# A gated mix of sliding attention and a GEGLU feed-forward: who makes the low parts of the hidden products

## The chip, the cores and the metric

The kernel runs on one core of a Trainium2 chip. The metric is the device time of one execution in microseconds (us). TensorE (PE) multiplies, VectorE (DVE) works on elements, ScalarE (ACT) copies and evaluates functions, GpSimd (POOL) and SyncE (SP) issue DMAs here. Each engine takes its instructions in the order of its own queue.

## The reference

```python
g = sigmoid((x * gate_w).sum(-1, keepdims=True))
a = attention(x, wqkv, wo)     # 32 heads of 16; query s sees keys s, s-2, ..., s-14; softmax; times wo
b = (gelu(x @ w_gate) * (x @ w_up)) @ w_down
out = g * a + (1 - g) * b
```

x has 2048 tokens of 512 channels, the feed-forward part (FFN) 1792 hidden features; all is float32.

## The kernel before

The tokens are taken in two parities (even and odd positions, `par` 0 and 1) of 1024 each, since the attention's step of 2 never mixes them. For each parity the program makes keys, queries and values, then the FFN in 14 chunks (`f`) of 128 hidden features. At the end of the second parity the results of the attention are multiplied by `wo` (`out_first` for the first parity, `finish` for the second) and the sums are stored.

Every float32 operand of a matmul is split: a high part is a rounded copy (`hh = Copy(ge)`), a low part what is left (`hl = ge - hh`), and a product is the sum of three matmuls, high by high, low by high and high by low. In the FFN the products of gate and up are made by a scheme of seven block products in place of eight. `gate_up` makes them for a chunk: PE's matmuls stand in line 781, ACT copies sums out of PSUM at L786, L792 and L867, DVE adds them at L793, ACT applies GELU at L882 and L898. PSUM has four banks with the tag `p` and four `acc` banks. `hidden` then multiplies GELU and up on DVE (L797) and makes the two parts, for two halves of the tokens per chunk. It has two ways. In the first, ACT makes the high part (L800) and DVE subtracts it (L801). In the second, ACT writes the negated value, rounded, to the low part (L805), POOL issues a DMA that adds the value to it in place (L806), and ACT makes the high part (L807). The table `LOWS` (line 40) names the chunks of each parity that take the second way. `down` multiplies the parts of earlier chunks by the down weights (PE L830); ACT brings half of the sums back into a PSUM bank before (L824) and out of it after (L845).

The attention is the filling. For each of 8 units (parity, 128 channels) DVE multiplies queries and keys (L539) and reduces (L542), subtracts the maximum (L553, L555), ACT takes the exponential (L557, with a load of its function table before it, and another before the next GELU), DVE normalizes (L562 to L568). `mix` then works through pairs of tokens: a product with the values `v` (L585), three additions (L589, L591, L593), and after every two pairs a transpose (L598), whose result goes to memory by SP (L600). The values come by L523 and L524 into one buffer. `channels` fetches a result from memory (L1040), ACT makes its high part (L90) and DVE its low part (L91). The two parts of `wo` are made at L135 (ACT) and L91. In `finish` PE multiplies them at L1062; ACT and DVE copy the sums out (L1111, L1109), SP stores them (L1115).

The order of all this is not written by hand: a scheduler lays out each engine's queue by its own estimate of when each instruction can run. The attention's instructions are handed in with a lower priority (`tc.high_priority(offset=-BEHIND)`), as many between two products as a budget allows (`pull`). There are six buffers each of `hh` and `hl`, and four `c` tiles hold GELU, up and their products.

Of the kernel before, what the change touches and what calls it, by code (L numbers as in the profile page):

```python
# [36 lines left out]
PIPE = 4  # L37
BT = 4
MASKED = -1e9 * DH ** 0.5
LOWS = (4, 8, 10), (4, 6, 8, 10, 12)  # L40


GROUPS = (("t1", "t2", "b11"), ("b21", "t3", "b22", "t4"))
# [5 lines left out]
def tile_gated_mix(ctx: ExitStack, tc: tile.TileContext, xt, wqkv, wff, wo, out):  # L49
# [11 lines left out]
    def tl(tag, dt=F32):  # L61
        return pool.tile([P, COLS.get(tag, 512)], dt, name=tag, bufs=BUFS[tag])
# [733 lines left out]
    def hidden(par, key, ge, up):  # L796
        nc.vector.tensor_tensor(ge, ge, up, op=OP.mult)  # L797
        hh_, hl_ = tl("hh", F32R)[:, :512], tl("hl", F32R)[:, :512]
        if key[0] not in LOWS[par]:
            END[:] = [nc.scalar.activation(hh_, ge, AF.Copy),  # L800
# [555 lines left out]
```

## Time and profile before

| | |
|---|---|
| time, median of 3 runs | 592.74 us (592.54 to 600.27) |
| profiled execution, time and span | 592.89 us, 591.1 us |
| PE busy | 585.7 us (99%) |
| DVE busy | 535.0 us (91%) |
| ACT busy | 425.3 us (72%) |
| POOL busy | 126.8 us (21%) |
| DMA | 141.71 MB, mean 240 GB/s |

The span is the time from the first to the last instruction that the profile holds; the profiled execution's own time is 1.79 us longer. In a row of the timeline the first number is the start in us from the span's start, the second the time until the end of the instruction, then engine, line, operation, result and operands; a bracket tells how long the engine was idle before it and what ended that. In a row of groups the numbers after the bar are the sum in us and the mean in ns.

### The profile page before, as it was taken

The page shows a single profiled execution, that of the slowest core. Times are in us where ns is not written, and L with a number is a line of the kernel's source. Part 1 is how long each engine was busy: PE and PEld are TensorE (multiplying, and loading weights), DVE is VectorE, ACT ScalarE, POOL GpSimd, SP SyncE. Part 2 cuts the span into 40 slices and gives each one's busy share as a digit, 9 for nine tenths or more (in the row PEclk, how much of TensorE's full clock was granted, in tenths as well). Part 3 has the DMA queues.
Part 4 walks back from the last instruction along what each step waited for, and adds up shares of the span by engine and source line. Part 5 has one row for each costly group of instructions (what it writes and reads, how often), then busy time and mean ns, then how long its engine had stood idle before and what let it go on. Part 6 is the DMA issues. An engine that isn't in the chain of part 4 may idle for free.

```text
span 591.1 us, 8266 instructions
## 1 busy us (share of the span) xinstructions
PE 585.7 (99%) x2743; PEld 489.1 (83%) x2743; DVE 535.0 (91%) x628; ACT 425.3 (72%) x752; POOL 126.8 (21%) x153
## 2 busy tenths in 40 slices
PE   9999999999999999999999999999999999999997
PEld 7889888888888888888889888888888888887885
DVE  6989998999899995998997999998999899989882
ACT  6778667778887779786687655768776967796522
POOL 0140751112111212113120761112121212112200
PEclk9999999999999999999999999999999999999999
DMA  8789999978987979899989999969798989548915
GB/s 305 228 247 281 301 310 231 296 197 238 289 222 218 273 205 273 224 264 347 284 231 380 222 272 269 277 162 257 178 263 224 254 213 247 144 111 227 202 44 178
DMA packets 87848, 141.71 MB, mean 240 GB/s; under 512 B 8575, under 2 KB 49919, under 8 KB 87806
## 3 DMA queue, kind: packets, MB, share of 16 engines
q1 hardware_dynamic: 65454, 103.21, 52.2%
q0 software_dynamic: 22064, 37.59, 34.6%
q8 instruction: 21, 0.34, 0.2%
q10 hardware_dynamic: 288, 0.39, 0.2%
q14 instruction: 21, 0.17, 0.1%
HBM read 69.83 MB, written 46.49 MB: 197 GB/s over the span
## 4 chain that ended last, share of the span: by engine, by line
PE 96%; ACT 2%; DMA 1%; issue 0%; SPq 0%; DVE 0%; ACTq 0%
PE p L781 44%; PE p L830 13%; PE acc L830 12%; PE acc L478 11%; PE p L1062 6%; PE p L364 4%; PE acc L364 3%; PE p L478 2%; PE acc L1062 2%; DMA raw<-xt 1%; ACT A L90 0%; ACT L898 0%; ACT g L135 0%; ACT hl L805 0%; ACT hh L807 0%
## 5 line engine op out<-in xcount | busy, mean ns | idle before, releaser
L781 PE MATMUL p<-S,g 128*128 128x512 f32 x672 | 167.0, 389 | 0.0
L781 PEld LDWEIGHTS p<-S,g 128*128 128x128 f32 x672 | 125.8, 188 | 25.8
L781 PE MATMUL p<-A,g 128*128 128x512 f32 x504 | 125.8, 389 | 0.0
L781 PEld LDWEIGHTS p<-A,g 128*128 128x128 f32 x504 | 94.4, 188 | 19.8 <-ACT rt L845 0.4
L585 DVE TENSOR_TENSOR prod<-v,lg 128x2048 f32<-128x2048 f32 x32 | 72.8, 2274 | 1.4 <-DMA v<-vs 1.2
L542 DVE TENSOR_REDUCE lg<-prod 128x128 f32<-128x2048 f32 x32 | 73.0, 2280 | 0.2
L539 DVE TENSOR_TENSOR prod<-kq 128x2048 f32<-128x2048 f32 x32 | 72.9, 2277 | 0.2
L830 PE MATMUL p<-d,hh 128*128 128x512 f32 x224 | 68.6, 390 | 0.3 <-ACT p L824 0.3
L830 PE MATMUL acc<-d,hh 128*128 128x512 f32 x224 | 59.7, 389 | 0.0
L740 POOL DMA_DIRECT2D g<-raw x26 | 23.6, 907 | 161.1 <-ACT g L737 103.6
L792 ACT ACTIVATE c<-p 128x512 f32<-128x512 f32 x56 | 33.4, 597 | 33.7 <-PE p L781 33.6
L830 PEld LDWEIGHTS p<-d,hh 128*128 128x128 f32 x224 | 41.9, 188 | 9.5 <-ACT p L824 0.8
L830 PEld LDWEIGHTS acc<-d,hh 128*128 128x128 f32 x224 | 42.0, 188 | 8.7
L793 DVE TENSOR_TENSOR c<-c,s 128x512 f32<-128x512 f32 x56 | 37.8, 681 | 5.5 <-ACT c L792 5.2
L830 PE MATMUL p<-d,hl 128*128 128x512 f32 x112 | 42.1, 389 | 0.0
L797 DVE TENSOR_TENSOR c<-c 128x512 f32<-128x512 f32 x56 | 38.1, 683 | 1.3 <-ACT c L898 1.2
L589 DVE TENSOR_TENSOR prod<-prod 128x1024 f32<-128x1024 f32 x32 | 39.0, 1217 | 0.1
L845 ACT ACTIVATE rt<-p 128x512 f32<-128x512 f32 x48 | 27.8, 596 | 15.0 <-PE p L830 14.8
L786 ACT ACTIVATE s<-p 128x512 f32<-128x512 f32 x56 | 33.2, 594 | 5.3 <-PE p L781 4.9
L478 PE MATMUL acc<-d,S 128*128 128x512 f32 x144 | 35.5, 390 | 0.1
L830 PE MATMUL acc<-d,hl 128*128 128x512 f32 x112 | 35.1, 389 | 0.0
L772 POOL DMA_DIRECT2D d<-r x23 | 19.8, 860 | 68.9 <-ACT d L771 41.6
(222 smaller groups left out, 1062.3 us busy)
## 6 DMA issues: line engine op xcount, KB each, us to landing
g<-raw POOLq DMA_DIRECT2D x26, 512.0 KB, 6.7
ws<-g SPq DMA_DIRECT2D x14, 768.0 KB, 5.9
g<-ws SPq DMA_DIRECT2D x14, 768.0 KB, 6.7
r<-wff SPq DMA_DIRECT2D x28, 256.0 KB, 4.4
raw<-wff SPq DMA_DIRECT2D x14, 512.0 KB, 4.6
d<-r POOLq DMA_DIRECT2D x23, 256.0 KB, 6.7
ws<-raw SPq DMA_DIRECT2D x14, 384.0 KB, 5.8
raw<-ws SPq DMA_DIRECT2D x14, 384.0 KB, 4.0
```

What stands on the lines that cost most here:

```text
L364: LAST[:] = [nc.tensor.matmul(ps[:, :n], x[:, ts], VO[b][w][:, kc * WQ:kc * WQ + n], start=first, stop=(kc == 1 and i == 2), skip_group_ch ...
L478: LAST[:] = [nc.tensor.matmul(ps, x[:, ts], w, start=(start and kc == i == 0), stop=(kc == 1 and i == 2), skip_group_check=True)]
L539: paced(nc.vector.tensor_tensor(prod, spans(k, jj), q[:, jj:jj + 2, None, :].to_broadcast([P, 2, W, UC]), op=OP.mult))
L542: nc.vector.tensor_reduce(two_of(lg, jj), prod.rearrange("p j w (h d) -> p (j w) h d", d=DH), axis=AX.X, op=OP.add)
L585: paced(nc.vector.tensor_tensor(prod.rearrange("p j w (h d) -> p (j w) h d", d=DH), spans(v, jj).rearrange("p j w (h d) -> p j w h d", d=D ...
L589: nc.vector.tensor_tensor(prod[:, :, :4], prod[:, :, :4], prod[:, :, 4:], op=OP.add)
L781: LAST[:] = [nc.tensor.matmul(ps, w_, a_, start=(start and kc == 0 and n == 0), stop=(kc == 1 and n == 2), skip_group_check=True)]
L792: nc.scalar.activation(c, ps, AF.Copy)
L793: nc.vector.tensor_tensor(c, c, s, op=OP.add)
L797: nc.vector.tensor_tensor(ge, ge, up, op=OP.mult)
L830: LAST[:] = [nc.tensor.matmul(pp, a[:, ts], w, start=(i == 0 and n == 0 and gr == 0), stop=(i == 1 and n == 2), skip_group_check=True)]
L1062: LAST[:] = [nc.tensor.matmul(pa, a, b, start=(first and n == 0), stop=(last and n == 2), skip_group_check=True)]
```

## The change

The table names no chunk of the second parity any more, so that there every chunk takes the first way of `hidden`.

```diff
-LOWS = (4, 8, 10), (4, 6, 8, 10, 12)
+LOWS = (4, 8, 10), ()
```

Five chunks with two halves make ten low parts. For each, the negated copy (L805) and the adding DMA (L806) go, the copy for the high part is L800 where it was L807, and DVE gets a subtraction (L801). The scheduler lays the queues out anew from chunk 4 of the second parity on; the order of all before is the same.

DVE's queue in the last chunk, from the last L801 on. In the names, `hl`, `hh` and `raw` are parts and data of results of the attention, `prod`, `o` and `tb` the steps of `mix`, `v_4789` and `v_4783` the values of the last unit but one, `v_5298` and `v_5288` those of the last unit. Before:

```order
L801 TENSOR_TENSOR hl_5351<-c_5347,hh_5350 128x512
L585 TENSOR_TENSOR prod_5202<-v_4789,lg_4287 128x2048
L91 TENSOR_TENSOR hl_5533<-raw_5530,hh_5532 128x4x4x32
L91 TENSOR_TENSOR hl_5568<-raw_5530,hh_5567 128x4x4x32
L91 TENSOR_TENSOR hl_5600<-raw_5530,hh_5599 128x4x4x32
L589 TENSOR_TENSOR prod_5202<-prod_5202 128x2x512
L591 TENSOR_TENSOR prod_5202<-prod_5202 128x2x256
L593 TENSOR_TENSOR o_5150<-prod_5202 128x4x64
L598 STREAM_TRANSPOSE tb_5033<-o_5150 128x512
L585 TENSOR_TENSOR prod_5303<-v_5298,lg_4792 128x2048
```

And now, the same place:

```order
L801 TENSOR_TENSOR hl_5341<-c_5337,hh_5340 128x512
L91 TENSOR_TENSOR hl_5523<-raw_5520,hh_5522 128x4x4x32
L598 STREAM_TRANSPOSE tb_5025<-o_5026 128x512
L585 TENSOR_TENSOR prod_5143<-v_4783,lg_4285 128x2048
L91 TENSOR_TENSOR hl_5558<-raw_5520,hh_5557 128x4x4x32
L91 TENSOR_TENSOR hl_5590<-raw_5520,hh_5589 128x4x4x32
L589 TENSOR_TENSOR prod_5143<-prod_5143 128x2x512
L591 TENSOR_TENSOR prod_5143<-prod_5143 128x2x256
L593 TENSOR_TENSOR o_5142<-prod_5143 128x4x64
L585 TENSOR_TENSOR prod_5193<-v_4783,lg_4285 128x2048
```

After the last row shown follow L589, L591, L593, L598 and then the first L585 on the last unit's values. So behind the last L801 there stands one more pair of the unit before the last, and one more transpose, and the three L91 have moved ahead of the L585 that frees the buffer of the values.

ACT's queue in the last chunk, from one L824 to the next (`p_5289` and `p_5279` are the bank of the first). Before:

```order
L824 ACTIVATE p_5289<-rt_3956 128x512
L786 ACTIVATE s_5235<-p_5179 128x512
L135 ACTIVATE S_5237<-raw_5048 128x512
L135 ACTIVATE S_5250<-raw_5048 128x512
L90 ACTIVATE A_5319<-raw_5262 128x4x4x32
L882 ACTIVATE c_5259<-p_5186 128x512
L90 ACTIVATE A_5337<-raw_5262 128x4x4x32
L805 ACTIVATE hl_5225<-c_5221 128x512
L807 ACTIVATE hh_5224<-c_5221 128x512
L824 ACTIVATE p_5324<-rt_3981 128x512
```

And now:

```order
L824 ACTIVATE p_5279<-rt_3956 128x512
L786 ACTIVATE s_5225<-p_5170 128x512
L135 ACTIVATE S_5227<-raw_5040 128x512
L557 ACT_TABLE_LOAD
L557 ACTIVATE lg_4786<-lg_4786 128x512
L135 ACTIVATE S_5240<-raw_5040 128x512
L90 ACTIVATE A_5309<-raw_5252 128x4x4x32
L882 ACT_TABLE_LOAD
L882 ACTIVATE c_5249<-p_5177 128x512
L90 ACTIVATE A_5327<-raw_5252 128x4x4x32
L800 ACTIVATE hh_5215<-c_5212 128x512
L824 ACTIVATE p_5314<-rt_3981 128x512
```

The exponential of the last unit (`lg_4786`) and the two table loads that go with it now stand between the two; before, the exponential stood 13 rows ahead of the first of them, the load back to GELU four rows ahead.

SP's queue at the end, as a difference (`os_134` is the last result of the attention, `s` and `rt` hold sums to be stored):

```order
 L1040 DMA raw<-os_133 128x512
 L600 DMA os_134<-tb 32x4x128 x4
-L1040 DMA raw<-os_134 128x512
 L1115 DMA out<-s 128x512
 L1115 DMA out<-rt 128x512
+L1040 DMA raw<-os_134 128x512
 L1115 DMA out<-s 128x512
 L1115 DMA out<-rt 128x512
```

The fetch of the last result now stands behind the first two stores of sums.

## The prediction

> **What bounds the kernel now.** I read the page's header and chain first, then the engines by stage, then the end of the span on VectorE (DVE), the DMA queue of SyncE (SP) and TensorE (PE).
>
> ```profile
> span 591.1 us, 8266 instructions
> PE 96%; ACT 2%; DMA 1%; issue 0%; SPq 0%; DVE 0%; ACTq 0%
> 350.00:550.00 200.00, 199.67 (x882) 164.98 (x881) 190.12 (x197) 148.79 (x247) 36.75 (x42) 1.00 0.85 219
> 550.00:591.00 41.00, 37.28 (x165) 30.54 (x163) 26.34 (x30) 14.91 (x25) 3.44 (x4) 1.00 0.53 138
> ```
>
> After the stretch and its length the columns are PE, PE's weight load, DVE, ScalarE (ACT), GpSimd (POOL), granted clock, DMA share and GB/s. Nearly the whole chain is matmuls, and in the stretch where the edit lies (350 to 550 us) PE misses 0.33 of 200 us at clock 1.00. So nothing that is taken off another engine there can bring more than 0.33 us. DVE is the second engine: busy 190.12 of 200 us, against ACT's 148.79. The edit loads the engine that is nearly full and relieves two that have room. The profiled execution took 592.89 us (1.79 outside the span), 0.15 over the median of 592.74; I sum against it.
>
> **What the edit removes and adds.** Chunks 4, 6, 8, 10 and 12 of the second parity have two GELU products each, so ten low parts change their way.
>
> ```profile
> L801 DVE TENSOR_TENSOR hl<-c,hh 128x512 fp32r<-128x512 f32 x40 | 27.2, 684 | 2.2 <-ACT hh L800 2.1
> L806 POOL DMA_DIRECT2D hl<-c x16 | 15.1, 942 | 83.1 <-ACT hl L805 82.8 <-DMA r<-wff 0.2
> L805 ACT ACTIVATE hl<-c 128x512 fp32r<-128x512 f32 x16 | 10.0, 628 | 0.0
> 450.22 1.29 DVE L801 TENSOR_TENSOR hl<-c,hh 128x512 fp32r<-128x512 f32 x2
> ```
>
> Removed: ten negated copies on ACT (0.63 us each by their row), ten POOL issues (0.94 us) and ten adding DMAs of 256 KB. All of it lay beside PE's work, POOL being busy 36.75 of 200 us and ACT 148.79, so I take the gain as 0, between 0 and the 0.33 us that PE misses. Added: ten subtractions of 0.684 us on DVE. Two in a row take 1.29 us together, so the second adds 0.60; ten are **6.0 us of DVE time**.
>
> The Trainium skill has a rule against such a step: "Perfetto Trace Analysis", section Optimizing Scalar/DVE Operations, says that some work may be better off on ScalarE when VectorE is saturated, which speaks against this edit. The trace agrees in part: VectorE at 190.12 of 200 us is near it, but with its 9.9 us idle not there, so by the rule alone the 6.0 us would fit and the sum would be 0.
>
> **Where the 6.0 us lie.** DVE is idle for 9.9 of the 200 us; three waits for the exponential of the attention hold most of what other work could fill.
>
> ```profile
> 411.55 0.69 DVE L562 TENSOR_REDUCE m<-lg 128x64 f32<-128x512 f32 x1 [2.22 <-ACT lg L557]
> 465.58 0.69 DVE L562 TENSOR_REDUCE m<-lg 128x64 f32<-128x512 f32 x1 [1.66 <-ACT lg L557]
> 520.41 0.69 DVE L562 TENSOR_REDUCE m<-lg 128x64 f32<-128x512 f32 x1 [1.44 <-ACT lg L557]
> ```
>
> They are 5.3 us. But DVE runs in its queue's order, and the change's order, with each row at its duration, has nearly the old amount of DVE work ahead of each FFN step (from 4 us less to 5 us more, mostly under 1.5), and the attention later instead. After the last L801 there now stand one more pair of tokens of mix (L585, L589, L591, L593) and one more transpose (L598) than before. I count that tail row by row.
>
> ```profile
> 543.48 0.69 DVE L801 TENSOR_TENSOR hl<-c,hh 128x512 fp32r<-128x512 f32 x1
> 544.08 2.28 DVE L585 TENSOR_TENSOR prod<-v,lg 128x2048 f32<-128x2048 f32 x1
> 546.28 1.89 DVE L91 TENSOR_TENSOR hl<-raw,hh 128x512 fp32r<-128x512 f32 x3
> 552.49 2.29 DVE L585 TENSOR_TENSOR prod<-v,lg 128x2048 f32<-128x2048 f32 x1 [1.25 <-DMA v<-vs]
> 557.26 2.29 DVE L585 TENSOR_TENSOR prod<-v,lg 128x2048 f32<-128x2048 f32 x1
> 569.83 0.69 DVE L91 TENSOR_TENSOR hl<-raw,hh 128x512 fp32r<-128x512 f32 x1 [0.89 <-ACT hh L90]
> 575.20 0.71 DVE L598 STREAM_TRANSPOSE tb<-o 128x512 f32<-128x512 f32 x1
> ```
>
> Before, the tail runs from 543.48 to 575.91, 32.4 us. A pair is 552.49 to 557.26, 4.8 us where nothing fills its bubbles. The last unit's v has one buffer: its load goes out when the L585 ahead of it ends (546.36) and is there at 552.49, 6.1 us later. Three L91 helped to fill that gap; in the new order they stand ahead of the L585, so the wait grows from 1.25 to about 2.9 us. Pair 4.8 (0.3 less where an L91 fills it), transpose 0.6, wait 1.65, less the wait of 0.89 at 569.83, which is covered now: 5.8 us, a **tail of 38.2 us**.
>
> **When the tail begins.** In the new order the exponential of the last unit with its two table loads sits between two L824 copies on ACT; before, it sat ahead of them.
>
> ```profile
> 518.46 1.28 ACT L557 ACT_TABLE_LOAD   x1
> 518.48 2.88 PE L781 MATMUL p<-A,g 128*128 128x512 f32 x12
> 519.75 0.63 ACT L557 ACTIVATE lg<-lg 128x512 f32<-128x512 f32 x1
> 522.33 0.58 ACT L867 ACTIVATE p<-p 128x512 f32<-128x512 f32 x1
> 524.52 1.28 ACT L898 ACT_TABLE_LOAD   x1
> 531.91 0.61 ACT L824 ACTIVATE p<-rt 128x512 f32<-128x512 f32 x1
> 539.27 0.60 ACT L898 ACTIVATE c<-p 128x512 f32<-128x512 f32 x1 [0.62 <-PE p L781]
> 532.57 0.72 PE L830 MATMUL p<-d,hh 128*128 128x512 f32 x2 [0.33 <-ACT p L824]
> 533.07 0.69 DVE L793 TENSOR_TENSOR c<-c,s 128x512 f32<-128x512 f32 x1 [0.97 <-ACT c L792]
> ```
>
> From L867 to the second L824 ACT took 9.58 us: one load of 1.29 and 16 steps of 0.52. Now there are two loads and 17 steps, 11.4 us. L867 can start when its product ends, at 518.48 + 2.88 = 521.36. The second L824 so starts at about 532.8, 0.9 us late, and PE, which already waited 0.33 us for it, **loses 0.9 us there**. Ends: 0, if ACT gets ahead earlier, and 3, if the copies in that stretch also wait for their loads from memory; nothing here shows that wait, so I take 0.9. DVE, behind ACT's copy just ahead of that L824, does an L801, a reciprocal and an L585 before the chunk's L793, then up to the last L801 eleven rows of about 0.60 (two L793, four L91, two L797, L568, L591, an L801), an L589 of 1.2 and two small ones of 0.5 together, 8.2 us: it starts at about 533.0 + 3.3 + 8.2 = 544.5, where it was 543.48. The last transpose ends at 544.5 + 38.2 = **582.7**, not 575.91.
>
> The Trainium skill would make the two loads dearer: "ScalarE: Activation LUTs", What ACT_TABLE_LOAD costs, gives 1.28 us for a load and 1.38 us for a drain. Here the exponential starts 1.29 us after the load at 518.46, so the trace shows the load and not the drain. By that rule two switches would add 2.8 us more, an estimate of 601 us instead of the forecast.
>
> **The end.** The last transpose feeds the last lowering matmuls by two DMAs.
>
> ```profile
> 575.94 1.75 SPq L600 DMA_DIRECT2D os<-tb  x4
> 579.16 0.34 SPq L1040 DMA_DIRECT2D raw<-os  x1
> 581.87 0.63 ACT L90 ACTIVATE hh<-raw 128x512 fp32r<-128x512 f32 x1 [0.75 <-DMA raw<-os]
> 582.53 0.69 DVE L91 TENSOR_TENSOR hl<-raw,hh 128x512 fp32r<-128x512 f32 x1 [6.62 <-ACT hh L90]
> 584.40 0.62 PE L1062 MATMUL p<-S,hh 128*128 128x512 f32 x2
> 586.89 0.39 PE L1062 MATMUL p<-S,hl 128*128 128x512 f32 x1
> 583.14 0.68 DVE L1109 COPY rt<-acc 128x512 f32<-128x512 f32 x1
> 583.86 0.34 SPq L1115 DMA_DIRECT2D out<-rt  x1
> ```
>
> Before, the high part was ready at 582.50 and PE came to its last 12 matmuls at 584.40: **1.9 us of slack**, which hides the first part of any delay. From the transpose's end to the issue of L1040 went 3.25 us, to the start of L90 another 2.7. So L1040 now goes out at about 586.0. There is a floor under it: SP's queue now holds two stores of results (L1115) ahead of this L1040, and they wait for PE's first two sums. The second sum's last matmul stands three places of 0.23 us ahead of the last 12 and takes 0.39: with the 0.9 us it ends at 585.0, and the copy (0.68) and the store's issue (0.34) make it 586.0 as well. Without the 0.9 us the floor is 585.1. Then L90 starts at 588.7, its low part (L91) ends at 590.0, and the third of the last 12 matmuls needs it: they count from 589.6 instead of 584.40. **+5.2 us**: span 596.3, time **598.1 us**, 0.9% over before.
>
> **Unknown costs.** The load of v, 6.1 us here, can be less with ten DMAs gone or more at another moment. The landing times of the loads into that tile:
>
> ```profile
> DMA to landing us min/median/max: 4.0/6.2/9.0
> ```
>
> That is 2 us either way, up to 2.9 more; downwards the floor at 585.1 stops it, at +4.3 us. PE's loss of 0 to 3 us moves the end by as much. Without PE's loss and with no queue floor (early stores) the tail alone would give 2 us. I take the middle values since they are the nearest rows. Own range of the forecast: 594.5 to 602.
>
> **The rivals.**
> *The gaps swallow it (not slower).* If DVE's queue fills its waits for the exponential (5.3 us) and the last transpose ends by 575.91 + 1.9 = 577.8, the end stays where it was: 592.9 us, at best 0.33 less. For it: the room of 9.9 us exceeds 6.0. Against: the order leaves one pair and one transpose more behind the last L801, whose own start hangs on ACT and PE; to come out even it would have to start at 577.8 - 38.2 = 539.6, where the last GELU itself (L898) starts only at 539.27, with a product and a copy between. It decides from there: the last L801 earlier than 540. Chance 0.09.
> *ACT's queue is blocked in many chunks (slower by over 2%).* ACT's L800 waits for DVE's product L797; where DVE comes late, the copies behind it that free PSUM banks come late, and PE with its four p banks stops, as at 532.57. DVE has up to 2.4 us more work ahead of some L793 and L797 (chunks 8 and 12). Nine chunks at about 1.0 us each on top of 5.2 make 607 us; it decides from some 0.75 us a chunk. Against: ACT is idle a quarter of the time and the L800 rows stand late in its queue. Chance 0.08.
>
> **How the numbers follow.** Forecast 0.80, swallowed 0.09, blocked 0.08; 0.03 is left for something unseen within 2%. Predicted time 598.1 us. The range 594.0 to 603.0 holds nearly all of the forecast's own range and a little of the blocked case; the swallowed case and most of the blocked one, under 0.2 together, lie outside. A difference of 2% (11.9 us, about what a measurement of this kernel can tell from no change) is passed on the slow side by the blocked case alone: slower 0.08. Faster by 2% would need 11.9 us from a PE that is idle 0.33 us in the stretch: 0.01. Within 2%: 0.91.
>
> **What would show each step.** The L801 group with 50 entries near 0.684 us and 6 of L806. The wait for v before an L585 near 555 to 562 us of about 2.9 us. A wait of PE for L824 near 532 of about 1.2 us in all. The last transpose ending near 582.7, the last L1040 issued near 586.0 behind two L1115, and PE idle some 4 us before its last 12 matmuls. Wrong if PE's idle time sits in the middle chunks, or if the last transpose ends before 578.

## The result, and the profile after

The changed kernel takes 600.67 us (median of 14 runs, 599.48 to 603.37), the kernel before 593.46 us in the same comparison (14 runs). The ratio is 1.0105, with a 95% interval of 1.0081 to 1.0129: 1.0% slower, too little to be told from no change by the 2% of the prediction, but clear of zero. The ratio is not the quotient of the two medians (1.0121), as it also weighs single runs that lie higher, as five of the 14 of the kernel before do (596.9 to 600.3 us). The changed kernel's profiled execution took 601.12 us, with a span of 599.2 us, 8.1 us more than before.

The page's header and chain, and then the engines by stage (columns as before: PE, weight load, DVE, ACT, POOL, granted clock, DMA share, GB/s):

```profile
span 599.2 us, 8240 instructions
PE 78%; DVE 9%; DMA 5%; issue 3%; ACT 2%; POOL 1%; SPq 0%; DVEq 0%; POOLq 0%; ACTq 0%
350.00:550.00 200.00, 199.96 (x882) 165.28 (x881) 191.39 (x204) 145.07 (x237) 28.34 (x32) 1.00 0.78 204
550.00:599.00 49.00, 39.91 (x164) 31.92 (x162) 31.45 (x34) 14.73 (x25) 3.44 (x4) 0.93 0.47 126
```

In the stretch of the edit PE misses nothing: 199.96 of 200 us. DVE did only 1.27 us more there (191.39 against 190.12), though it was given 6.0 us of subtractions. The rest is work of the attention that moved behind 550 us: DVE does 31.45 us there, where it did 26.34. The chain is no longer PE alone. It now holds 9% DVE and 5% DMA, and the clock after 550 us is 0.93 instead of 1.00.

The tail on DVE, then SP, ACT and PE at the end, from the timelines:

```profile
543.45 0.68 DVE L801 TENSOR_TENSOR hl<-c,hh 128x512 fp32r<-128x512 f32 x1
560.07 2.29 DVE L585 TENSOR_TENSOR prod<-v,lg 128x2048 f32<-128x2048 f32 x1 [3.50 <-DMA v<-vs]
581.79 0.71 DVE L598 STREAM_TRANSPOSE tb<-o 128x512 f32<-128x512 f32 x1
585.13 0.36 SPq L1115 DMA_DIRECT2D out<-rt  x1
585.75 0.33 SPq L1040 DMA_DIRECT2D raw<-os  x1
589.35 0.63 ACT L90 ACTIVATE hh<-raw 128x512 fp32r<-128x512 f32 x1 [4.48 <-DMA raw<-os]
590.03 1.22 PE L1062 MATMUL p<-S,hh 128*128 128x512 f32 x2 [5.61 <-ACT hh L90]
594.89 0.63 PE L1062 MATMUL p<-S,hl 128*128 128x512 f32 x1
```

Before, PE came to its last 12 matmuls at 584.40 and did not wait. Now it is ready at 584.42 (590.03 less 5.61) and waits 5.61 us. And the matmuls themselves have become slower: two took 0.62 us, now 1.22. The view of stages, of before and then of the changed kernel, shows why:

```profile
584.40:587.20 2.80, 2.80 (x13) 2.06 (x11) 1.38 (x2) 1.11 (x2) 0.00 (x0) 1.00 0.87 336
```

```profile
590.00:595.60 5.60, 5.49 (x12) 3.76 (x12) 1.38 (x2) 1.24 (x3) 0.00 (x0) 0.50 0.24 94
```

The granted clock is 0.50 in the whole of these 5.5 us. From the first of the last 12 matmuls to the start of the last went 2.49 us before (584.40 to 586.89) and go 4.86 us now. So the last matmul starts 8.0 us later: the first of the 12 comes 5.63 us later, and the way from there to the last takes 2.37 us more. Not all of the 2.37 us is the clock. The third of the 12 needs the low part, which DVE makes (L91) after the high part; three runs below that wait only briefly and keep the clock at 1.00 take 2.88 to 2.91 us for the 12. So some 0.4 us is the late low part, and some 2.0 us (4.86 less 2.90) the clock.

### The profile page after: what moved, and what is told of

It is laid out like the page before. It is cut to its first block, busy times and chain, and to the rows that moved or that the text cites. A ratio compares the mean times of both kernels' runs of the same rounds, so it can differ in the third digit from the quotient of the medians.

```text
span 599.2 us, 8240 instructions
## 1 busy us (share of the span) xinstructions
PE 588.6 (98%) x2743; PEld 490.8 (82%) x2743; DVE 541.2 (90%) x638; ACT 421.2 (70%) x742; POOL 118.1 (20%) x143
## 4 chain that ended last, share of the span: by engine, by line
PE 78%; DVE 9%; DMA 5%; issue 3%; ACT 2%; POOL 1%; SPq 0%; DVEq 0%; POOLq 0%; ACTq 0%
PE p L781 42%; PE acc L830 11%; PE p L830 10%; PE acc L478 7%; PE acc L364 3%; PE p L364 3%; DVE prod L585 1%; DMA ws<-g 1%; DMA os<-tb 1%; DVE prod L589 1%; DMA g<-vwt 1%; DVE S L91 1%; DMA raw<-os 1%; PE p L1062 1%; PE p L478 1%
## 5 line engine op out<-in xcount | busy, mean ns | idle before, releaser
L585 DVE TENSOR_TENSOR prod<-v,lg 128x2048 f32<-128x2048 f32 x32 | 72.8, 2274 | 3.8 <-DMA v<-vs 3.5
L792 ACT ACTIVATE c<-p 128x512 f32<-128x512 f32 x56 | 33.4, 597 | 35.0 <-PE p L781 34.9
L793 DVE TENSOR_TENSOR c<-c,s 128x512 f32<-128x512 f32 x56 | 37.9, 682 | 5.5 <-ACT c L792 5.0
L797 DVE TENSOR_TENSOR c<-c 128x512 f32<-128x512 f32 x56 | 38.2, 683 | 2.0 <-ACT c L898 2.0
L589 DVE TENSOR_TENSOR prod<-prod 128x1024 f32<-128x1024 f32 x32 | 39.0, 1218 | 0.1
L801 DVE TENSOR_TENSOR hl<-c,hh 128x512 fp32r<-128x512 f32 x50 | 34.1, 684 | 2.6 <-ACT hh L800 2.6
```

The source lines that it names most:

```text
L585: paced(nc.vector.tensor_tensor(prod.rearrange("p j w (h d) -> p (j w) h d", d=DH), spans(v, jj).rearrange("p j w (h d) -> p j w h d", d=D ...
L589: nc.vector.tensor_tensor(prod[:, :, :4], prod[:, :, :4], prod[:, :, 4:], op=OP.add)
L792: nc.scalar.activation(c, ps, AF.Copy)
L793: nc.vector.tensor_tensor(c, c, s, op=OP.add)
L801: nc.vector.tensor_tensor(hl_, ge, hh_.bitcast(F32), op=OP.subtract)]
```

## The experiments

The theory after the result, A: the ten subtractions hurt nowhere in the chunks. They push DVE's last attention steps back, beyond PE's slack of 1.9 us, and PE's wait then also halves its clock. The rivals: B, the subtractions by themselves take PE's time, wherever they stand; C, the end has little to do with it. The expectations use B and D also for narrower rivals, which they state. In the table "wait" is PE's wait before the last 12 matmuls, "12" the time from the first of these to the start of the last, both from the profile; the ratio is to the kernel before.

| kernel | median us | ratio, 95% interval | last transpose ends | wait | 12 |
|---|---|---|---|---|---|
| before | 593.46 | 1 | 575.91 | 0 | 2.49 |
| after | 600.67 | 1.0105 (1.0081 to 1.0129) | 582.50 | 5.61 | 4.86 |
| warm_end | 603.02 | 1.0144 (1.0103 to 1.0185) | 582.36 | 3.42 | 4.11 |
| warm_long | 605.25 | 1.0182 (1.0146 to 1.0218) | 582.96 | 0.47 | 2.90 |
| v_in_kq | 600.02 | 1.0102 (1.0065 to 1.0140) | 580.60 | 4.70 | 4.67 |
| v_stores | 597.67 | 1.0059 (1.0031 to 1.0087) | 580.29 | 2.72 | 4.03 |
| v_stores_warm | 596.48 | 1.0061 (1.0046 to 1.0075) | 580.66 | 0.27 | 2.91 |
| b_late | 598.17 | 1.0081 (1.0056 to 1.0107) | 579.24 | 3.16 | 4.21 |
| lows_12 | 601.47 | 1.0135 (1.0121 to 1.0150) | 584.35 | 5.34 | 4.86 |
| lows_4to10 | 598.35 | 1.0089 (1.0068 to 1.0111) | 579.07 | 2.48 | 4.17 |
| l4to10_vkq | 592.20 | 1.0017 (0.9990 to 1.0045) | 575.54 | 0 | 2.49 |
| pool_low | 594.07 | 1.0024 (1.0014 to 1.0034) | 577.14 | 0.27 | 2.88 |
| b_v_in_kq | 592.94 | 0.9998 (0.9976 to 1.0020) | 579.20 | 0 | 2.49 |

**Lateness of the tail alone.** The kernel before, with the product of the first two pairs of tokens of the last unit made twice on DVE, and no edit of the table:

```diff
+            for _ in range(2 if (par, u) == (1, NU - 1) and jj < 4 else 1):
                 paced(nc.vector.tensor_tensor(prod...
```

> The kernel before, with ten low parts by DMA as ever, but in the last unit two products of values and weights (L585 of before) are made twice, 4.5 us more on VectorE behind the last GELU product. Theory A: lateness of the tail alone brings the loss: last transpose near 580.4, last fetch at the queue floor near 585.1, TensorE waits some 4.5 us and runs the last 12 at half clock; the time rises from 592.8 to about 599.5. Theory C (the ten subtractions spread over the chunks are what costs): the time stays near 592.8 to 593.5.

The end of its timelines, DVE, SP and PE (its lines stand one further down):

```profile
578.53 0.71 DVE L599 STREAM_TRANSPOSE tb<-o 128x512 f32<-128x512 f32 x1
583.74 0.33 SPq L1041 DMA_DIRECT2D raw<-os  x1
587.41 1.10 PE L1063 MATMUL p<-S,hh 128*128 128x512 f32 x2 [3.16 <-ACT hh L90]
```

With all ten DMAs in place, attention steps that end 3.3 us later cost 0.81%, some 4.8 us. The median, 598.17 us, is less than the 599.5 expected, as the last transpose came at 579.24 and not at 580.4, but far from the 592.8 to 593.5 of C. C falls. The loss is more than the lateness less the slack, by the slow clock (12 matmuls in 4.21 us) and by the stores that again stand ahead of the fetch.

**The wait for v, and SP's queue.** First the last unit's v goes into a kq buffer that is free by then, then the first four stores of sums also leave SP's queue for POOL's:

```diff
-        VT[par, u] = v = pool.tile([P, 2 * NP - 1, UC], F32, name="v")
+        if (par, u) == (1, NU - 1):
+            v = pool.tile([P, 3 * NP - 1, UC], F32, name="kq")[:, :2 * NP - 1]
...
-            cols = ... else ((nc.sync, 0, 512),)
+            cols = ... else ((nc.gpsimd if jj < 4 else nc.sync, 0, 512),)
```

> The changed kernel, with the last unit's values loaded into the free buffer of keys and queries, so that the load need not wait for the unit before. Theory A with the queue floor (SyncE's queue holds two stores ahead of the last fetch): the wait of 3.5 us before the last unit's first product goes, the last transpose ends near 579.0 instead of 582.5, but the last fetch goes out at about 585.1 instead of 585.75, behind the stores; the time falls by 0.6 us only, to about 600.1. Without such a floor: the time falls by 3.5 us, to about 597, or by 5.9 if the clock then holds. Theory C (VectorE's load in the middle chunks costs the time): no change.

> As e2_v_in_kq, and the first four stores of results go through GpSimd's queue, so that the last fetch stands behind none. Theory A: last transpose near 579.0, last fetch at about 582.3, TensorE back at about 586.5 after a wait of some 2.2 us; the time falls by 3.5 us to about 597.2, and to 594.8 if a wait that short leaves the clock at full. Theory C: no change against the changed kernel.

The end of v_in_kq (DVE, SP, PE; its lines stand four further down) and then of v_stores, there with two rows of the engine view:

```profile
579.89 0.71 DVE L602 STREAM_TRANSPOSE tb<-o 128x512 f32<-128x512 f32 x1
584.66 0.43 SPq L1119 DMA_DIRECT2D out<-rt  x1
585.59 0.33 SPq L1044 DMA_DIRECT2D raw<-os  x1
589.44 1.22 PE L1066 MATMUL p<-S,hh 128*128 128x512 f32 x2 [4.70 <-ACT hh L90]
```

```profile
579.58 0.71 DVE L602 STREAM_TRANSPOSE tb<-o 128x512 f32<-128x512 f32 x1
583.83 0.34 SPq L1044 DMA_DIRECT2D raw<-os  x1
587.15 1.22 PE L1066 MATMUL p<-S,hh 128*128 128x512 f32 x2 [2.72 <-ACT hh L90]
585.00:588.00 3.00, 0.85 (x2) 0.62 (x3) 0.85 (x2) 0.63 (x1) 1.42 (x3) 0.80 0.90 346
588.00:590.00 2.00, 2.00 (x6) 1.60 (x6) 0.00 (x0) 0.60 (x1) 0.00 (x0) 0.50 0.30 119
```

In v_in_kq the last transpose ends 1.9 us earlier, not the 3.5 us of the wait, mainly because DVE there waits 0.83 and 0.36 us for high parts from ACT. The fetch goes out only 0.16 us earlier: the two stores hold it, the floor under L1040 is real. Without them ahead it goes out 1.76 us earlier still, and the time falls by 2.35 us. Both times came close to what was expected (600.1 and 597.2 us), though the last transposes ended 1.6 and 1.3 us later than the 579.0 expected. But 0.6% is left, with the last 12 matmuls in 4.03 us.

**The clock.** Small matmuls (128x128, bf16, on a tile of zeros that lies there anyway) into a bank that is free by then, ahead of the last 12, to keep PE busy while it waits; their sums are overwritten.

```diff
             if jj < BT:
                 add(NU - 2, BT + jj)
+            if jj == BT:
+                idle = bank("acc0")
+                for _ in range(42):                       # 95 in warm_long, 46 in v_stores_warm
+                    tc.keep_in_program_order(nc.tensor.matmul(idle[:, :P], warm, warm, ...))
```

> The changed kernel with 42 small matmuls of zeros (128x128, bf16, into the free bank acc0) ahead of TensorE's last 12 matmuls, so that TensorE does not stand idle there. Theory A (the end: the last transpose is late, TensorE waits 5.6 us, and after the wait its clock is at half for the last 12 matmuls): the last 12 take 2.7 us again instead of 5.5, and the time falls by about 2.5 us, from 600.7 to 598.2. Theory B (the last 12 matmuls are slow for another reason, such as operands that come late): the time stays within 0.5 us of 600.7.

> As e1_warm_end with 95 small matmuls in place of 42: those 42 took 2.5 us and left TensorE a wait of 3.4 us, so 95 take 5.7 us and fill the whole wait. Theory A (the half clock comes from the wait): the last 12 matmuls take 2.7 us in place of 5.5 and the span falls from 599.2 to about 596.6. Theory B (operands): the last 12 stay at 5.5 us. A third outcome, small matmuls that don't hold the clock: the last 12 stay slow although TensorE never stood idle.

> As e3_v_stores, with 46 small matmuls ahead of the last 12 to fill the wait of 2.7 us left there. Theory A: without the half clock the last 12 take 2.7 us in place of 4.4; the span falls from 595.6 to about 594, the time from 597.7 to about 596.

PE at the end of warm_end, of warm_long (with two rows of the engine view for PE alone: length, PE busy, clock, DMA share, GB/s) and of v_stores_warm:

```profile
584.28 2.50 PE L1105 MATMUL acc<-warm 128*128 128x128 bf16 x42
590.21 1.22 PE L1062 MATMUL p<-S,hh 128*128 128x512 f32 x2 [3.42 <-ACT hh L90]
```

```profile
585.00 5.46 PE L1105 MATMUL acc<-warm 128*128 128x128 bf16 x95
590.94 0.73 PE L1062 MATMUL p<-S,hh 128*128 128x512 f32 x2 [0.47 <-ACT hh L90]
593.84 0.39 PE L1062 MATMUL p<-S,hl 128*128 128x512 f32 x1
590.00:592.00 2.00, 1.52 (x12) 1.00 0.06 22
592.00:594.00 2.00, 2.00 (x10) 1.00 0.17 67
```

```profile
587.66 0.73 PE L1066 MATMUL p<-S,hh 128*128 128x512 f32 x2 [0.27 <-ACT hh L90]
590.57 0.39 PE L1066 MATMUL p<-S,hl 128*128 128x512 f32 x1
```

The first was badly sized: 42 of them last only 2.50 us, and the 3.42 us of waiting behind them brought the slow clock back. With 95 the wait is 0.47 us, and the last 12 run at clock 1.00, 2.90 us in place of 4.86. So it is the wait that halves the clock, and not the kind of matmul or the DMAs at that time. On v_stores the same step takes 1.1 us off the last 12 (4.03 to 2.91) and 1.2 us off the median; its ratio, 1.0061, cannot be told from the 1.0059 without it, since the two were compared with different runs of the kernel before.

The times of warm_end and warm_long missed what was expected. warm_end took 603.02 us in the median where 598.2 was expected. warm_long's span was to fall to 596.6 us; its profile has 598.1, as the last fetch went out 0.45 us later than in the changed kernel and took 4.06 us to L90, not 3.60; its median time is 605.25 us. Both profiles show the shortest of six executions (600.52 and 600.13 us); what the others lose, and where, no profile shows. So these two runs show what the wait does to the clock, but as a cure the extra matmuls failed.

**More and fewer low parts by the DMAs.** The table keeps the adding DMAs for chunk 12 alone (eight more subtractions than before), or for chunks 4, 6, 8 and 10 (two more, in chunk 12):

```diff
-LOWS = (4, 8, 10), ()
+LOWS = (4, 8, 10), (12,)             # lows_12
+LOWS = (4, 8, 10), (4, 6, 8, 10)     # lows_4to10
```

> The changed kernel with the low parts of chunk 12 made by adding DMAs again: eight more subtractions than before, in chunks 4 to 10. Theory A (what counts is the whole of VectorE's time up to the last transpose, wherever it is added): eight times 0.60 are 4.8 us, less what the gaps take; the last transpose comes some 4 us late, TensorE waits and loses its clock, the time is 597 to 600. Theory D (the subtractions near the end, those of chunk 12, cost): close to before, 592.8 to 594.

> The counterpart: chunks 4 to 10 by adding DMAs as before, chunk 12 by VectorE, two subtractions more than before. Theory A: 1.2 us more, which the 1.9 us of slack before the last 12 matmuls hides: 592.8 to 593.8, with TensorE waiting under 1 us. Theory D: nearly all of the loss, 597 or more.

PE, DVE and PE in lows_12:

```profile
393.98 2.11 PE L830 MATMUL acc<-d,hh 128*128 128x512 f32 x8 [1.15 <-ACT hh L800]
561.58 2.29 DVE L585 TENSOR_TENSOR prod<-v,lg 128x2048 f32<-128x2048 f32 x1 [3.99 <-DMA v<-vs]
593.41 1.22 PE L1062 MATMUL p<-S,hh 128*128 128x512 f32 x2 [5.34 <-ACT hh L90]
```

With eight the end is as with ten, and the time, 601.47 us, lies above the 597 to 600 that A gave. Its profiled execution, the longest of the six (604.46 us), also shows that a chunk can be hit: PE waits 1.15 us for ACT's high part at 394, which waits for DVE's product, and 1.06 us at 536 for a copy by ACT (L792) that frees a bank. That is what the second rival feared, twice and not in nine chunks.

DVE (the first three rows; the first is the L585 that frees the buffer of v) and PE in lows_4to10:

```profile
545.43 2.28 DVE L585 TENSOR_TENSOR prod<-v,lg 128x2048 f32<-128x2048 f32 x1
555.33 2.29 DVE L585 TENSOR_TENSOR prod<-v,lg 128x2048 f32<-128x2048 f32 x1 [3.95 <-DMA v<-vs]
578.36 0.71 DVE L598 STREAM_TRANSPOSE tb<-o 128x512 f32<-128x512 f32 x1
586.28 1.22 PE L1062 MATMUL p<-S,hh 128*128 128x512 f32 x2 [2.48 <-ACT hh L90]
```

This one was missed: two subtractions, 1.2 us of DVE, cost 0.89%, some 5.3 us. That is what D gave, but lows_12, which leaves chunk 12 to the DMAs, loses as much as ten do. The last L801 of lows_4to10 starts at 543.29, before it was 543.48, so it is not the sum of DVE's work that is late. The wait for v has grown from 1.25 to 3.95 us. About half of that is the order: two L91 stand ahead of the L585 that frees the buffer, as in the changed kernel three do, and it ends at 547.71 where it ended at 546.36. The other half is the load itself: from there to the first use 7.6 us pass, before it was 6.1; why is not known (in pool_low below, with the old order at this place, it is 7.3). So A was put too simply: what counts is when the attention's last steps end, not how much is subtracted. So the same kernel once more, with v in the kq buffer (the edit above):

> The second parity's chunks 4, 6, 8 and 10 keep the adding DMAs (only chunk 12 is subtracted by VectorE, two more subtractions than before), and the last unit's v goes into a kq buffer that is free by then, so that its load need not wait for the last use of the v before it. Without the second step this kernel's profile had a wait of 3.95 us for v and its last transpose ended at 579.07. Theory A (what costs is where the new order puts the last attention steps, above all the three L91 ahead of the product that frees v's buffer, and then TensorE's slow clock): the wait goes, the last transpose ends at 575.1 to 576, within the slack, and the time is 592.5 to 594. Theory B (the two subtractions near the end cost by themselves, whatever waits for v): the time stays at 596 to 598.

DVE and SP at its end; the L589 is the first product with the last unit's v, and has no wait:

```profile
551.11 2.25 DVE L589 TENSOR_TENSOR prod<-kq,lg 128x2048 f32<-128x2048 f32 x1
574.83 0.71 DVE L602 STREAM_TRANSPOSE tb<-o 128x512 f32<-128x512 f32 x1
579.10 0.34 SPq L1044 DMA_DIRECT2D raw<-os  x1
```

The wait is gone, the last transpose ends at 575.54, PE does not wait, and the median is 592.20 us. DVE's order at this place is that of lows_4to10, with the two L91 ahead of the product that frees the old buffer; only the last unit's buffer differs. Two subtractions more cost nothing that can be measured, once v is not late. Its 12 runs lie between 591.72 and 598.92 us, which widens its interval. It is ahead of the changed kernel, not of the kernel before.

**A third maker of the low parts.** GpSimd subtracts them; neither the DMAs nor more DVE work:

```diff
-                      nc.vector.tensor_tensor(hl_, ge, hh_.bitcast(F32), op=OP.subtract)]
+                      (nc.gpsimd if par and key[0] in (4, 6, 8, 10, 12) else nc.vector).tensor_tensor(
+                          hl_, ge, hh_.bitcast(F32), op=OP.subtract)]
```

> The changed kernel with the ten low parts of the five chunks subtracted by GpSimd: neither adding DMAs nor more VectorE work. What a GpSimd subtraction takes and whether it slows VectorE no run has shown. Its order has, behind the last L801, the same pairs and transposes as the kernel before, the three L91 behind the product that frees v's buffer, and the last fetch ahead of the stores. Theory A (the order of the attention's last steps decides): last transpose at 575 to 577, time 592.5 to 594. Rival (the low parts come later or VectorE is slowed while GpSimd computes, so that TensorE waits in the chunks): over 596, with TensorE's missing time between 350 and 550 us.

Its subtractions on POOL (shortest, median and longest in ns, first and last start), the last transpose, and PE's last matmuls (lines from L1063 on stand one further down):

```profile
L801 POOL TENSOR_TENSOR hl<-c,hh x10: 1288/2263/4242, 402.7 to 530.3; 128x512 fp32r<-128x512 f32 x10
576.43 0.71 DVE L598 STREAM_TRANSPOSE tb<-o 128x512 f32<-128x512 f32 x1
583.94 0.73 PE L1063 MATMUL p<-S,hh 128*128 128x512 f32 x2 [0.27 <-ACT hh L90]
```

One takes 2.26 us (median) where DVE needs 0.684, and PE waits 0.27 us in all at the end. It costs 0.24% against the kernel before, with the adding DMAs gone as in the changed kernel. The last transpose, 577.14, and the median, 594.07 us, lie a little above what A gave (577 and 594). The last matmul starts at 586.82, before it was 586.89; its span, 592.2 us, is 1.1 us longer behind that, where only copies and stores are left. So the loss of the changed kernel is not in giving up the DMAs, but in what DVE's queue then does at the end.

**The control.** v in the kq buffer in the kernel before:

> The kernel before with the last unit's v in a free kq buffer. Theory A: its last transpose ends up to 1.25 us earlier (the wait for v goes), which lies within the slack of 1.9 us ahead of the last matmuls: 592.5 to 593.5, no difference that can be measured. Rival (the attention's last steps bound the kernel before as well): up to 1.3 us faster, 591.6.

No difference: 0.9998. The attention's last steps do not bound the kernel before. Its profiled execution, 596.73 us, is the longest of its 12: PE comes to the last 12 matmuls 3.85 us later than before, so its last transpose says nothing of the slack. It shows by chance what the removed way of making low parts can do: PE waits for an adding DMA, and the clock drops behind that wait too, to 0.50 between 413 and 415 us. First the row of PE, then the engine view with PE alone (length, PE busy, clock, DMA share, GB/s):

```profile
412.24 1.98 PE L834 MATMUL acc<-d,hl 128*128 128x512 f32 x4 [1.89 <-DMA hl<-c]
410.00:430.00 20.00, 18.11 (x73) 0.91 0.78 191
```

## Why the prediction was right, and where not

The forecast was 598.1 us, its range 594.0 to 603.0. The result, 600.67, lies within, and the likeliest case is the one that happened. But the sum put the last matmul 5.2 us late, and it came 8.0 us late; the range was wide enough for that. By its steps:

- *Ten subtractions, 6.0 us of DVE time.* Right: the group of L801 has 50 entries now, 670/684/693 ns; L806 has 6.
- *One pair and one transpose more in the tail, the wait for v at 2.9 us.* Right in kind, its size 0.85 us too small: the wait is 3.50 us, and the tail from 543.45 to 582.50 is 39.05 us, against the 38.2 counted. Most of the difference is the load of v, which took 6.7 us from the end of the L585 ahead of it (553.39) to the first use (560.07), where 6.1 were counted. v_in_kq shows the wait's share: without it the last transpose ends 1.9 us earlier. The row of that L585:

```profile
551.10 2.29 DVE L585 TENSOR_TENSOR prod<-v,lg 128x2048 f32<-128x2048 f32 x1
```

- *The tail begins at 544.5, and PE loses 0.9 us at L824.* Wrong in its anchor. ACT's stretch from L867 to the second L824 is 11.53 us, 11.4 were counted:

```profile
520.26 0.58 ACT L867 ACTIVATE p<-p 128x512 f32<-128x512 f32 x1
531.79 0.60 ACT L824 ACTIVATE p<-rt 128x512 f32<-128x512 f32 x1
532.44 0.73 PE L830 MATMUL p<-d,hh 128*128 128x512 f32 x2
```

  But L867 starts 1.1 us before the 521.36 that the prediction took for the end of its product. That was the end of a row of 12 matmuls, which holds two products of six; L867 needs the first. So L824 comes no later than before, PE's 0.9 us are not lost, and the last L801 starts at 543.45. That the last transpose still came at 582.50, where 582.7 was forecast, is luck: this miss cancelled with the tail, 0.85 us longer than counted.
- *L1040 at 586.0, by the tail and by SP's queue alike.* Right: 585.75, behind two L1115. v_in_kq shows the floor, v_stores what it is worth.
- *2.7 us from L1040 to L90.* Too little: 3.60 us, 0.65 us net of the 0.25 us that L1040 was early. With the last 12 matmuls at clock 1.00 (2.90 us, as in warm_long), the last of them would start at 592.93, where the sum put it at 592.09: 0.84 us late, mostly by this.
- *The last 12 matmuls take what they took.* This is **the term that was missing**. The prediction saw "PE idle some 4 us" and let the matmuls behind it run at clock 1.00; they ran at 0.50, and the last started at 594.89, another 1.96 us later. 5.2 + 0.84 + 1.96 = 8.0 us, which is what the last matmul is late.

The first rival, gaps that swallow the work, needed the last L801 before 540; it started at 543.45. l4to10_vkq and pool_low show that this case exists once the last transpose ends near 577 or before. The second, ACT's queue blocked in many chunks, would have shown between 350 and 550 us, where PE misses 0.04 us.

For the missing term the trace of before had no row, since PE never waits there for long. The Trainium skill has it, in "TensorE: Matmul & The Clock Gate", Part 1: The HAM clock gate: after one idle window or more of about 3.4 us the clock falls to half, and it comes back after about 3.4 us of sustained work. The traces agree with the half. They agree with the return only in part: 0.50 ended at about 590.2 in v_stores, 3.05 us after PE started again (by the mean of 0.95 between 590 and 592), but in the changed kernel it held for all 5.5 us of the last 12 matmuls. The fall can come earlier here: waits of 2.72 us (v_stores), 2.48 us (lows_4to10) and even 1.89 us (b_v_in_kq) sufficed.

## What to carry to other kernels

Where work is added to an engine that is not the bound, don't ask only whether it has room, but what its queue does last: here 6 us of subtractions vanished among the chunks, and came back as attention steps behind the last chunk, one buffer's reload and one DMA queue behind them. When PE is the bound and comes to wait for some 2 us or more, as it did here, count its next matmuls at half the clock (an estimate from these profiles), for some 3 us behind a wait of 2 to 3.5 us, and for 4 to 6 us behind one of 4.7 us or more. And the same subtractions can cost 5.3 us or nothing that can be measured, by whether a load waits for one buffer (lows_4to10, 598.35 us, and l4to10_vkq, 592.20 us): find the instruction that frees the buffer in the order before counting the work.

## What was not expected of the hardware

- PE's clock after a wait: 0.50 for about 3 to 5.5 us of matmuls behind waits of 2.48 to 5.61 us, 0.91 on average over the 20 us around a wait of 1.89 us, and 1.00 behind waits of 0.27 and 0.47 us.
- The half clock lasted some 3.4 us in four profiles (v_stores: 586.7 to 590.2) and some 6.8 us, twice that, in three (the changed kernel: 589.1 to 595.9; v_in_kq and lows_12 likewise), by the granted clock in steps of 0.5 us. It began 2.3 us after PE stopped in v_stores and 4.7 us after in the changed kernel. The three are those with the longest waits (4.70 to 5.61 us), the four had 2.48 to 3.42 us.
- The fetch L1040 takes longer from its issue to L90 when two stores have been issued shortly ahead of it on SP's queue: 2.99 to 4.06 us in the six profiles with them (3.60 in the changed kernel), 2.61 to 2.98 us in the six without where the fetch ended the wait. That the stores cause it was not tried by itself.
- A GpSimd subtraction of 128x512 took 2.26 us in the median (1.29 to 4.24), 3.3 times DVE's, and DVE's sums of gate and up (L793) took 702 ns in that kernel where they take 681.
